# Exps as shifted piecewise linear powers on VectorE, streamed FFN weights and column-tiled matmuls in a transformer block

## Chip, cores and metric

The kernel runs on one core of one Trainium2 chip. The metric is device time in microseconds (us) of one execution. The time before is 918.04 us (median of 3 runs, 917.89 to 921.31). Every experiment was run with executions of the kernel before beside it on the same chip. All executions quoted were classed as fast.

## The reference

One adaLN block: layer norm, modulation from `c`, attention with 32 heads of width 16 over 2048 tokens, residual, second layer norm, FFN with a tanh GELU gate, residual. Cut to what matters:

```python
x = A_x                                        # (1, 2048, 512) bf16
mod = (silu(c) @ w_mod)                        # six rows of 512
h = layernorm(x) * (1 + ca) + sa
q, k, v = split(h @ wqkv)                      # 32 heads, 16 wide
p = softmax(q @ k.T * 16 ** -0.5)              # 32 x 2048 x 2048 exps
x = x + ga * ((p @ v) @ wo)
h = layernorm(x) * (1 + cb) + sb
x = x + gb * ((gelu(h @ w_gate) * (h @ w_up)) @ w_down)   # 512 -> 1792 -> 512
```

## The kernel before

Scores are made transposed: keys on 128 partitions, 512 queries along the free axis. One such 128x512 tile in one PSUM bank is called a **slot** here. There are 32 x 16 x 4 = 2048 slots to exponentiate. ScalarE takes two or three slots per activation. Some single slots go to VectorE instead. PV is a matmul of `[v, 1]` (17 columns, so that the softmax denominator comes out with it), and four heads run side by side in four column tiles of TensorE. A **round** is such a group of four slots.

Tokens are worked off in groups of 512, 512, 512, 256, 128, 128 (called groups 0 to 5). While the attention of one group runs, the output projection, layer norm and FFN of the group before are fed into TensorE's gaps as "side work". All side work shares one PSUM bank, `mi`. The order of everything is fixed when the program is built, by a greedy scheduler with a model of time of its own; it is not decided on the chip.

```python
    def mm(self, out, lhsT, rhs, start=True, stop=True, tp=None):      # all matmuls pass here
        n = 1
        for _, k in rhs.ap[1:]:
            n *= int(k)
        n *= 4 if mybir.dt.size(rhs.dtype) == 4 else 1
        return self.rec("pe", lambda e: e.matmul(out, lhsT, rhs, start=start, stop=stop, tile_position=tp),
                        [lhsT, rhs], [out], cost=(n, int(rhs.ap[0][1]), tp))

    def exp_dve(self, i, bank):                # one slot on VectorE: five operations
        t, lo, u, out = self.dt[i % 2], self.dlo[i % 2], self.du[i % 2], self.ED[:, i % 3, :]
        return [lambda: self.ts("dve", t, bank, 127 * OCT, 0.0, ALU.add, ALU.max),
                lambda: self.stt(u, lo, EXP_C2 / EXP_C3 * OCT, lo, ALU.add, ALU.mult),
                lambda: self.stt(u, u, (EXP_C1 - 1) / EXP_C3 * OCT ** 2, lo, ALU.add, ALU.mult),
                lambda: self.ts("dve", t.bitcast(FP32), t, 128 / OCT, None, ALU.mult),
                lambda: self.stt(out.bitcast(I16), u, 128 * EXP_C3 / OCT ** 3, t.bitcast(FP32), ALU.mult,
                                 ALU.add)], out

    def mod_cols(self, bank, base):            # modulation columns: 32 matmuls of ONE column
        for ci in range(8):
            for dc in range(NDC):
                self.mm(bank[:, ci:ci + 1], self.wmod[:, dc, base + P * ci:base + P * ci + P],
                        self.sc_bf[:, dc:dc + 1], start=(dc == 0), stop=(dc == NDC - 1))

    # ... FFN of one group (cut): gate chunk G, up chunk U; chunks of 256 of the 1792 columns
        def G(ci):
            # ... four or eight matmuls into mi ...
            self.copy("dve", g[...], mi[...])
            self.task([lambda: self.tt("dve", w, g, g, ALU.mult),
                       lambda: self.ts("dve", w, w, GELU_C, 1.0, ALU.mult, ALU.add),
                       lambda: self.tt("dve", w, w, g, ALU.mult),
                       ("act", lambda: self.act(w, w, ACT.Tanh, scale=TANH_C0))], ("gelu", gi, ci))
    # ... the weights are loaded once (wg, wu, wd; 5.5 MB) and stay in SBUF ...

    # ... in stream(): when a slot may go to VectorE
                if (('v', 3, 0) in self.have and len(active) < NACT and ... and self.backlog() < BACK
                        and self.free["dve"] < t + 700 and len(mem) == CH and slack > -100 and self.credit < 1024):
    # credit: matmul columns of side work that are owed by now
```

The softmax here doesn't subtract the row's maximum and nothing guards it: scores larger than these inputs give would overflow.

## Time and profile before

| | before |
|---|---|
| time, median | 918.04 us |
| slots on ScalarE / on VectorE | 1891 / 157 |
| filler matmuls (whole 128x128x512, to keep TensorE's clock up) | 312 |

The profile's busy table, kernel before. Each entry is an engine, its busy us, its share of the span and its instructions:

```profile
PE 806.3 (88%) x7461; PEld 262.4 (29%) x7461; DVE 773.6 (84%) x1512; ACT 890.1 (97%) x747; POOL 3.6 (0%) x11
```

The chain of waits that ended last, by engine, kernel before:

```profile
ACT 87%; PE 6%; DVE 5%; DMA 1%; SPq 0%; issue 0%; DVEq 0%
```

ScalarE (ACT) is busy 97% of the span and carries 87% of the chain. It is the bound.

Groups of instructions, kernel before: line of a helper, engine, operation, output <- inputs, shapes, count, then busy us and mean ns of one, then idle time before it and who ended it:

```profile
L310 ACT ACTIVATE E<-ps_sc 128x1536 bf16<-128x1536 f32 x507 | 732.0, 1603 | 2.1 <-PE ps_sc L297 1.8
L310 ACT ACTIVATE E<-ps_sc 128x1024 bf16<-128x1024 f32 x185 | 214.1, 1175 | 1.1 <-PE ps_sc L297 1.1
L322 DVE TENSOR_SCALAR dt<-ps_sc 128x512 int32<-128x512 f32 x157 | 108.4, 690 | 45.8 <-PE ps_sc L297 43.8
L327 DVE SCALAR_TENSOR_TENSOR ED<-du,dt 128x512 int16<-128x512 f32 x157 | 106.9, 683 | 0.6
```

Durations of neighbours overlap at their ends. A three-slot activation lasts 1.60 us, but in the chain of waits 18 of them in a row take 24.18 us, 1.34 us each. That spacing is what one costs; for two slots it is 0.92 us. So the exps cost ScalarE 507 x 1.34 + 185 x 0.92 = 850 us.

Busy us by stretch, kernel before. Columns: stretch, its length, then busy us and instruction counts of PE, PEld, DVE, ACT and POOL, then TensorE's granted clock, the DMA share and GB/s:

```profile
0.00:100.00 100.00, 87.86 (x740) 34.33 (x740) 67.98 (x174) 89.14 (x85) 3.65 (x11) 0.95 0.34 108
100.00:650.00 550.00, 477.33 (x3464) 128.81 (x3461) 497.37 (x901) 548.99 (x453) 0.00 (x0) 1.00 0.06 18
650.00:800.00 150.00, 135.66 (x1550) 43.76 (x1547) 128.21 (x245) 149.96 (x122) 0.00 (x0) 1.00 0.07 17
800.00:900.00 100.00, 90.14 (x1530) 44.08 (x1525) 70.95 (x171) 97.45 (x81) 0.00 (x0) 1.00 0.07 16
```

From 100 to 880 us ScalarE is full; before that it waits for the start, after that for the tail.

TensorE's timeline of the kernel before, start and duration in us; these lines show what a change of mode costs:

```profile
399.79 0.39 PE L297 MATMUL ps_sc<-qT,kme 32*128 32x512 bf16 x3
400.11 0.39 PE L297 MATMUL ps_mi<-wreg,mreg 128*128 128x512 bf16 x1
...
410.38 0.39 PE L297 MATMUL ps_pv<-E,vaug 128*17 128x512 bf16 x3
410.39 0.38 PE L297 MATMUL ps_pv<-ED,vaug 128*17 128x512 bf16 x1
410.60 0.39 PE L297 MATMUL ps_pv<-E,vaug 128*17 128x512 bf16 x4
```

Two PV rounds in the same mode start 0.22 us apart. A row-tiled score round and a whole matmul start 0.32 us apart. The Trainium skill gives a reason, in "TensorEngine Tiling (Array Packing)", "Key Properties": changing the tiling mode drains TensorE. The trace agrees that a change costs time, here 0.10 us; it doesn't show the draining itself.

### The profile page before, as it was taken

The numbers are of one execution on the slowest core, as the hardware profiler recorded it, in microseconds if no ns is written. First come the engines' busy times: TensorE is split into PE (matmuls) and PEld (weight loads), VectorE is DVE, ScalarE is ACT, GpSimd is POOL, SyncE is SP. The second block draws the span as 40 slices with busy tenths as digits, with TensorE's granted clock in tenths as the row PEclk, the third lists the DMA queues.
The fourth block names the chain that finished last, engine by engine and source line by source line (L and its number), as shares of the span: only waits on it lengthen the run. The fifth ranks groups of instructions, "written<-read, shape, count | busy, mean of one in ns | idle before, by whom it ended". The sixth has DMA issues, their size and how long they took to land.

```text
span 919.3 us, 17768 instructions
## 1 busy us (share of the span) xinstructions
PE 806.3 (88%) x7461; PEld 262.4 (29%) x7461; DVE 773.6 (84%) x1512; ACT 890.1 (97%) x747; POOL 3.6 (0%) x11
## 2 busy tenths in 40 slices
PE   7999888888889888888898888888889989998987
PEld 3333222222222222222222222222222322334455
DVE  7746999989897999998997999999999787868664
ACT  5999999999999999999999999999999999999992
POOL 1000000000000000000000000000000000000000
PEclk8899999999999999999999999999999999999999
DMA  9002320000000000000000000000000000000000
GB/s 297 1 25 55 132 93 13 13 14 14 14 13 5 10 12 14 14 13 17 16 19 12 14 13 13 2 13 18 25 21 14 14 8 14 26 20 14 21 8 13
DMA packets 31417, 24.97 MB, mean 27 GB/s; under 512 B 16205, under 2 KB 26122, under 8 KB 31338
## 3 DMA queue, kind: packets, MB, share of 16 engines
q1 hardware_dynamic: 28954, 22.28, 8.4%
q10 hardware_dynamic: 2384, 1.57, 0.6%
q8 instruction: 58, 0.95, 0.4%
q14 instruction: 21, 0.17, 0.1%
HBM read 21.23 MB, written 2.61 MB: 26 GB/s over the span
## 4 chain that ended last, share of the span: by engine, by line
ACT 87%; PE 6%; DVE 5%; DMA 1%; SPq 0%; issue 0%; DVEq 0%
ACT E L310 84%; PE ps_sc L297 3%; ACT wreg L310 2%; PE ps_mi L297 1%; PE ps_pv L297 1%; DVE du L327 1%; DMA scr_rec<-rden 1%; DVE st L350 0%; DVE dt L322 0%; DMA rb<-scr_rec 0%; SPq L360 0%; DVE xw L314 0%; DVE nwt L314 0%; DVE hreg L322 0%; PE ps_mi L301 0%
## 5 line engine op out<-in xcount | busy, mean ns | idle before, releaser
L310 ACT ACTIVATE E<-ps_sc 128x1536 bf16<-128x1536 f32 (+2 forms) x698 | 863.9, 1481 | 11.9 <-PE ps_sc L297 11.5
L297 PE MATMUL ps_pv<-E,vaug 128*17 128x512 bf16 (+2 forms) x2499 | 180.5, 325 | 1.3 <-DVE vaug L331 1.1
L297 PE MATMUL ps_sc<-qT,kme 32*128 32x512 bf16 (+2 forms) x1344 | 155.6, 332 | 23.2 <-ACT E L310 17.5
L297 PE MATMUL ps_sc<-qT,kmo 32*128 32x512 bf16 (+2 forms) x1408 | 154.4, 324 | 19.5 <-ACT E L310 15.3
L322 DVE TENSOR_SCALAR dt<-ps_sc 128x512 int32<-128x512 f32 x157 | 108.4, 690 | 45.8 <-PE ps_sc L297 43.8
L297 PE MATMUL ps_mi<-wreg,mreg 128*128 128x512 bf16 (+2 forms) x512 | 127.2, 340 | 11.4 <-DVE wreg L327 7.0
L297 PE MATMUL ps_sc<-xs,ident 128*128 128x512 bf16 x285 | 92.3, 386 | 42.2 <-ACT E L310 40.2
L327 DVE SCALAR_TENSOR_TENSOR ED<-du,dt 128x512 int16<-128x512 f32 x157 | 106.9, 683 | 0.6
L327 DVE SCALAR_TENSOR_TENSOR du<-du,dt 128x512 f32<-128x512 f32 x157 | 106.0, 681 | 0.3
L327 DVE SCALAR_TENSOR_TENSOR du<-dt 128x512 f32<-128x512 uint16 x157 | 106.1, 683 | 0.2
L297 PEld LDWEIGHTS ps_sc<-qT,kme 32*128 32x128 bf16 x1344 | 41.4, 91 | 138.0 <-ACT E L310 93.3
L297 PEld LDWEIGHTS ps_sc<-qT,kmo 32*128 32x128 bf16 x1408 | 42.2, 91 | 129.0 <-ACT E L310 85.8
L297 PEld LDWEIGHTS ps_pv<-E,vaug 128*17 128x17 bf16 x2499 | 48.8, 88 | 101.2 <-issue 90.9
L297 PE MATMUL ps_mi<-dreg,hreg 128*128 128x512 bf16 x210 | 65.3, 385 | 1.7 <-DVE xw L314 1.0
L322 DVE TENSOR_SCALAR dt<-dt 128x512 f32<-128x512 int32 x157 | 64.9, 417 | 0.6
L297 PEld LDWEIGHTS ps_mi<-wreg,mreg 128*128 128x128 bf16 x512 | 38.9, 97 | 76.9 <-issue 35.8
L297 PE MATMUL ps_pv<-ED,vaug 128*17 128x512 bf16 (+2 forms) x189 | 59.6, 346 | 0.3 <-DVE ED L327 0.2
L331 DVE CAST wreg<-ps_mi 128x512 bf16<-128x512 f32 x51 | 35.1, 688 | 17.7 <-PE ps_mi L297 16.9
L297 PEld LDWEIGHTS ps_sc<-xs,ident 128*128 128x128 bf16 x285 | 19.5, 97 | 90.4 <-ACT E L310 88.0
L327 DVE SCALAR_TENSOR_TENSOR wreg<-wreg,ps_mi 128x512 bf16<-128x512 bf16 x51 | 34.8, 683 | 7.3 <-PE ps_mi L297 7.1
L297 PE MATMUL ps_mi<-hreg,wreg 128*128 128x512 bf16 x120 | 39.2, 390 | 1.6 <-DVE qT L322 0.9
L297 PE MATMUL ps_mi<-wo,onorm 128*128 128x512 bf16 x120 | 36.5, 384 | 0.7 <-DVE xw L314 0.7
(116 smaller groups left out, 506.4 us busy)
## 6 DMA issues: line engine op xcount, KB each, us to landing
rb<-scr_rec SPq DMA_DIRECT2D x96, 64.0 KB, 2.0
mreg<-in_w_mod_dram SPq DMA_DIRECT2D x1, 2048.0 KB, 14.5
out_dram<-xs SPq DMA_DIRECT2D x16, 128.0 KB, 1.7
mreg<-in_B_w_gate_dram SPq DMA_DIRECT2D x4, 448.0 KB, 3.9
mreg<-in_B_w_up_dram SPq DMA_DIRECT2D x4, 448.0 KB, 5.4
rb<-scr_rec SPq DMA_DIRECT2D x52, 32.0 KB, 1.8
dreg<-in_B_w_down_dram SPq DMA_DIRECT2D x3, 512.0 KB, 5.2
wreg<-in_A_wqkv_dram SPq DMA_DIRECT2D x3, 384.0 KB, 10.6
```

The costliest lines, as they stand in the source:

```text
L297: return self.rec("pe", lambda e: e.matmul(out, lhsT, rhs, start=start, stop=stop, tile_position=tp), [lhsT, rhs], [out], cost=(n, int(rhs ...
L310: return self.rec("act", lambda e: e.activation(out, in_, func, scale=scale, **kw), rd, wr, cost=self.cost("act", out, [in_], "act"))
L322: return self.rec(eng, lambda e: e.tensor_scalar(out, a, s1, s2, **kw), rd, [out], cost=self.cost(eng, out, [a], "ts"))
L327: return self.rec("dve", lambda e: e.scalar_tensor_tensor(out, a, s, b, op0=op0, op1=op1), rd, [out], cost=self.cost("dve", out, [a, b], " ...
L331: return self.rec(eng, lambda e: e.tensor_copy(out, in_), [in_], [out], cost=self.cost(eng, out, [in_], "ts"))
```

## The change

Intent: take more exps off ScalarE. On VectorE a slot's exp becomes one read of the scores that writes the 16-bit pattern of a piecewise linear power of two. Its error is evened out by summing five such powers, shifted against each other. The four shifted copies are cheap 16-bit additions over a whole round (2048 elements). The sum is taken by TensorE: each shifted copy is one more PV round against a rescaled copy of V, accumulated in the same PSUM bank. Only key tiles 12 to 15 may be done so, because the scaled copies of V (`vs`) need SBUF. To make room, FFN weights are streamed anew for groups 0 to 3, and for groups 4 and 5 they are reloaded into space that has come free; the ring of ScalarE's exps shrinks from 15 slots to 12. TensorE gets four more PV rounds per VectorE round. To pay for that, every whole matmul becomes four column tiles, so that it shares PV's mode.

The diff, cut to its core (cuts marked `...`):

```diff
-NSL = 15
+NSL = 12
+T0 = 12
+NK = 3
+CREDIT = 1024
...
+SHIFT = (26, 51, 77, 102)
+SHIFT_C = float(128 * (127 - np.log2(5) - 0.0565))
...
+        if tp is None and int(rhs.ap[0][1]) == P and int(lhsT.ap[-1][1]) == P and mybir.dt.size(rhs.dtype) == 2:
+            for j in range(4):
+                self.mm(out[32 * j:32 * j + 32], lhsT[:, 32 * j:32 * j + 32], rhs, start, stop, (0, 32 * j))
+            return
         return self.rec("pe", lambda e: e.matmul(out, lhsT, rhs, start=start, stop=stop, tile_position=tp),
...
+        def load(x, ci):                       # streamed: next chunk of w_gate / w_up
+            if flow and ci < len(chunks):
+                self.dma("sp", self.wst[x][ci % 2], v[:, :, 2 * P * ci:2 * P * ci + 2 * P], "st%d%d" % (x, ci % 2))
...
-        due = (ends[1] + 30, ends[2] + 30, ends[3] + LAG, ends[-2] - 16)
+        due = (ends[1] + 30, ends[2] + 30, ends[3] + LAG, ends[3] + 2 * LAG)
...
+            if parts and pos >= loaded and ("ffn", 2 if early else 3) in self.have:    # reload for groups 4, 5
...
+                    elif (cand and self.quad_free and (pos < ends[2] or self.credit < CREDIT) and ...):
+                        ...                    # a new round of four slots for VectorE
+                    self.ts("dve", kq[:, 512 * j:512 * j + 512].bitcast(U16), self.scp[:, s0 + n, :], 128 / OCT, SHIFT_C,
+                            ALU.mult, ALU.add)
...
+    def shift_task(self, q, i):
+            self.ts("dve", self.sq[s].bitcast(U16), self.kq[q["k"]].bitcast(U16), float(SHIFT[i]), None, ALU.add)
```

`pos < ends[2] or credit < CREDIT`: after the attention of group 2 (slot 1536 of 2048), a VectorE round starts only while little side work is owed.

## The prediction

> **What bounds it now.** ScalarE. The busy table has ACT 97%, PE 88%, DVE 84%; the chain of waits is 84% ScalarE exps; in the table of stretches ACT is busy 50.0 of 50 us nearly everywhere from 100 to 850 us. The exps are 2048 slots of 128x512: by the groups of instructions 507 three-slot and 185 two-slot activations take about 1891, VectorE 157. In the chain a three-slot activation costs 1.34 us, a two-slot one 0.92: 850 us. Around that: 16 us before the first exp, 38 us after the last, 24 us of FFN tanh; ScalarE's waits are small (11.5 us on scores).
>
> **VectorE exps.** Today a slot costs five operations; in the timeline four start 0.60 us apart, the fifth takes 0.33: 2.73 us. After, a slot is one read of scores (0.60), plus, per round of four slots, four 2048-element 16-bit shifts. The bf16 1024-element tensor_scalar takes 414 ns, the two-tensor form 684, which agrees with the Trainium skill, "VectorE: DVE Perf Modes", "The perf-mode tier table" (4x for bf16 tensor_scalar in SBUF). From 291 ns at 512 elements and 414 at 1024 I estimate 0.66 us for 2048, 0.60 start to start. A round then costs 4.8 us instead of 10.9.
>
> **How many rounds n go to VectorE.** Its other work is 356 us of durations by the groups, about 300 start to start. Only k-tiles 12 to 15 are allowed (120 rounds at most). Usage near 0.83 of 850 us leaves about 402 us: n = 84 (75 to 100), 335 slots instead of 157. Each goes with a two-slot activation: 335 x 0.92 + (1713 - 670)/3 x 1.34 = 774 us of ScalarE against 850: 76 us less, all on the critical path.
>
> **TensorE.** Added: four PV rounds per VectorE round, 0.22 us each (two started 410.38 and 410.60): 73 us. Removed: most fillers (312, some 78 us with their switches), and mode switches between PV and full matmuls. A change of mode costs 0.1 us (score round to FFN matmul 0.32, same mode 0.22), as in the skill, "TensorEngine Tiling (Array Packing)", "Key Properties": switching drains. Five such per 12 us: 35 to 40 us. Four concurrent column tiles should take as long as one full matmul. So PE ends above 90% of a shorter span, and ScalarE's waits for scores should grow by 10 to 25 us: E has 12 slots instead of 15, and a unit's PV can't end until VectorE's last shift, which blocks the next unit in the one PV bank.
>
> **Off the path.** Streaming weights: some 16 MB more at a mean of 26 GB/s now, landings of 2 to 5 us: no cost. Scaled copies of V: 4 us of VectorE. The tail stays about 38 us.
>
> **Sum.** 918 - 76 + about 15 of new waits = 857. I say 856 us, range 828 to 890. Faster by over 2%: 0.91; within 2%: 0.06; slower: 0.03.
>
> **What would show it.** ScalarE exp time down by about 75 us; about 335 VectorE score reads and as many shifts at about 0.66 us; PE at 90% or more, fillers below 100; column-tiled FFN groups 0.22 us apart; DVE 85 to 92%; ACT over 93%.
>
> **What would make it wrong.** The unsigned 16-bit shift not getting the fast mode (1.2 or 2.2 us): n collapses. Column tiles loading weights slower (four loads for one), making PE the bound: 880 or more. VectorE late with shifts, filling E and stalling ScalarE. Or the scheduler reaching n near 110: about 830.

## The result and the profile after

The changed kernel takes 907.09 us (median of 4 runs, 904.66 to 909.09), against 919.67 us for the kernel before in the same rounds. The ratio is 0.986, 95% interval 0.983 to 0.989. Ratios here are the mean time of one kernel's fast runs over that of the other's of the same rounds, so not quite the ratio of the medians quoted. The range of the prediction (828 to 890) is missed.

The busy table and the chain of waits by engine, changed kernel:

```profile
PE 817.2 (90%) x13408; PEld 288.4 (32%) x13408; DVE 687.5 (76%) x1303; ACT 841.9 (93%) x747; POOL 3.7 (0%) x11
```

```profile
ACT 51%; PE 31%; DMA 7%; DVE 7%; SPq 3%; issue 2%; DVEq 0%
```

ScalarE's share of the chain fell from 87% to 51%. TensorE, DMA and the queue of the sync engine (SPq) have come in, and so has "issue", time in which an engine waits for nothing that the profile shows.

Groups of instructions, changed kernel (`dreg` and `mreg` hold the VectorE exps now):

```profile
L322 ACT ACTIVATE E<-ps_sc 128x1536 bf16<-128x1536 f32 x384 | 545.0, 1508 | 17.6 <-PE ps_sc L309 16.5
L322 ACT ACTIVATE E<-ps_sc 128x1024 bf16<-128x1024 f32 x308 | 310.7, 1096 | 4.9 <-PE ps_sc L309 4.6
L334 DVE TENSOR_SCALAR dreg<-ps_sc 128x512 uint16<-128x512 f32 x188 | 129.5, 690 | 36.0 <-PE ps_sc L309 34.0
L334 DVE TENSOR_SCALAR mreg<-ps_sc 128x512 uint16<-128x512 f32 x92 | 63.0, 689 | 16.0 <-PE ps_sc L309 15.0
L334 DVE TENSOR_SCALAR mreg<-dreg 128x2048 uint16<-128x2048 uint16 x188 | 123.1, 682 | 2.8 <-PE ps_pv L309 2.8
```

VectorE takes 188 + 92 = 280 slots (70 rounds). The prediction had 335. The shift of 2048 elements takes 0.68 us; the prediction had 0.66. The Trainium skill, "VectorE: DVE Perf Modes", "The perf-mode tier table", gives 693 ns for a bf16 tensor_scalar of that size in the 4x mode. The trace agrees, for uint16. At the spacings of before, ScalarE's exps now cost 384 x 1.34 + 308 x 0.92 = 798 us: 52 less, where the prediction had 76.

Busy us by stretch, changed kernel, columns as above:

```profile
0.00:100.00 100.00, 80.27 (x1540) 32.41 (x1540) 57.67 (x161) 79.18 (x77) 3.67 (x11) 0.93 0.25 80
100.00:650.00 550.00, 522.24 (x6860) 155.65 (x6856) 490.75 (x836) 546.47 (x494) 0.00 (x0) 1.00 0.13 35
650.00:800.00 150.00, 133.24 (x2440) 50.63 (x2441) 87.25 (x180) 145.17 (x115) 0.00 (x0) 0.98 0.31 89
800.00:900.00 100.00, 81.06 (x2583) 49.73 (x2580) 49.81 (x125) 71.11 (x64) 0.00 (x0) 0.95 0.25 68
```

From 100 to 650 us the picture is the predicted one: ScalarE full, VectorE at 89%, TensorE at 95%. Before 100 us ScalarE loses 10 us against the kernel before. After 650 us VectorE falls to 58% and then 50%, and ScalarE is no longer full.

To see what each stage gained, I counted slots: the moment by which ScalarE's activations and VectorE's reads have done so many of the 2048. The stages of each profiled execution in us:

| profiled run | to slot 160 | 160 to 1536 | 1536 to 2048 | after slot 2048 | span |
|---|---|---|---|---|---|
| before | 91.1 | 574.4 | 230.5 | 23.3 | 919.3 |
| after | 100.1 | 527.5 | 246.4 | 30.5 | 904.5 |
| change | +9.0 | -46.9 | +15.9 | +7.2 | -14.8 |

The middle stage won 47 us. The start, the last quarter of the slots and the tail gave 32 of them back.

### The profile page after: what moved, and what is told of

It reads as the page before. It is cut to its first block, busy times and chain, and to the rows that moved or that the text cites. A ratio compares the mean times of both kernels' runs of the same rounds, so it can differ in the third digit from the quotient of the medians.

```text
span 904.5 us, 29537 instructions
## 1 busy us (share of the span) xinstructions
PE 817.2 (90%) x13408; PEld 288.4 (32%) x13408; DVE 687.5 (76%) x1303; ACT 841.9 (93%) x747; POOL 3.7 (0%) x11
## 3 DMA queue, kind: packets, MB, share of 16 engines
HBM read 43.25 MB, written 2.61 MB: 51 GB/s over the span
## 4 chain that ended last, share of the span: by engine, by line
ACT 51%; PE 31%; DMA 7%; DVE 7%; SPq 3%; issue 2%; DVEq 0%
ACT E L322 49%; PE ps_mi L309 13%; PE ps_sc L309 12%; PE ps_pv L309 6%; DMA scr_rec<-rden 3%; SPq L372 3%; ACT wreg L322 2%; DMA mreg<-in_B_w_gate_dram 1%; DVE mreg L334 1%; DMA mreg<-in_w_mod_dram 1%; DVE wreg L326 1%; DVE wreg L339 1%; DVE wreg L343 1%; DMA rb<-scr_rec 1%; DMA mreg<-in_B_w_down_dram 1%
## 5 line engine op out<-in xcount | busy, mean ns | idle before, releaser
L322 ACT ACTIVATE E<-ps_sc 128x1536 bf16<-128x1536 f32 (+2 forms) x698 | 811.6, 1318 | 35.2 <-PE ps_sc L309 33.9
L309 PE MATMUL ps_sc<-qT,kmo 32*128 32x512 bf16 (+2 forms) x1408 | 183.8, 328 | 10.8 <-ACT E L322 7.5
L309 PE MATMUL ps_sc<-qT,kme 32*128 32x512 bf16 (+2 forms) x1344 | 178.0, 333 | 14.4 <-ACT E L322 12.1
L334 DVE TENSOR_SCALAR dreg<-ps_sc 128x512 uint16<-128x512 f32 x188 | 129.5, 690 | 36.0 <-PE ps_sc L309 34.0
L309 PE MATMUL ps_mi<-wreg,mreg 128*32 128x512 bf16 (+2 forms) x1920 | 124.1, 355 | 17.4 <-DVE wreg L339 5.4
L334 DVE TENSOR_SCALAR mreg<-dreg 128x2048 uint16<-128x2048 uint16 x188 | 123.1, 682 | 2.8 <-PE ps_pv L309 2.8
L309 PE MATMUL ps_pv<-mreg,vs 128*17 128x512 bf16 (+1 forms) x1232 | 98.4, 361 | 1.9 <-DVE mreg L334 1.4
L334 DVE TENSOR_SCALAR mreg<-ps_sc 128x512 uint16<-128x512 f32 x92 | 63.0, 689 | 16.0 <-PE ps_sc L309 15.0
L309 PEld LDWEIGHTS ps_mi<-wreg,mreg 128*32 128x32 bf16 x1920 | 42.8, 98 | 73.9 <-issue 26.0
L334 DVE TENSOR_SCALAR mreg<-mreg 128x2048 uint16<-128x2048 uint16 x92 | 60.3, 684 | 0.9 <-PE ps_pv L309 0.9
L343 DVE CAST wreg<-ps_mi 128x512 bf16<-128x512 f32 x51 | 35.0, 686 | 23.9 <-PE ps_mi L309 23.3
L309 PE MATMUL ps_mi<-hreg,wreg 128*32 128x512 bf16 x480 | 39.9, 391 | 0.7 <-DVE vaug L343 0.5
L326 DVE TENSOR_TENSOR onorm<-osb,rb 128x512 bf16<-128x512 f32 (+2 forms) x43 | 23.6, 549 | 19.8 <-DMA rb<-scr_rec 19.6
L309 PE MATMUL ps_mi<-mreg,hreg 128*32 128x512 bf16 x448 | 36.5, 384 | 0.2 <-DMA mreg<-in_B_w_down_dram 0.2
```

What stands on the lines that cost most here:

```text
L322: return self.rec("act", lambda e: e.activation(out, in_, func, scale=scale, **kw), rd, wr, cost=self.cost("act", out, [in_], "act"))
L326: return self.rec(eng, lambda e: e.tensor_tensor(out, a, b, op), [a, b], [out], cost=self.cost(eng, out, [a, b], "tt"))
L334: return self.rec(eng, lambda e: e.tensor_scalar(out, a, s1, s2, **kw), rd, [out], cost=self.cost(eng, out, [a], "ts"))
L343: return self.rec(eng, lambda e: e.tensor_copy(out, in_), [in_], [out], cost=self.cost(eng, out, [in_], "ts"))
```

## The experiments

Eighteen kernels ran. Medians; "before" is the median of before in the same rounds, and the ratio is as explained above:

| label | this us | before us | ratio |
|---|---|---|---|
| e_small | 889.65 | 918.84 | 0.967 |
| e_tile256 | 898.89 | 918.84 | 0.978 |
| e_untiled | 907.88 | 918.84 | 0.987 |
| b_tile256 | 924.00 | 918.84 | 1.006 |
| s_poolw | 891.20 | 919.47 | 0.969 |
| s_gate_open | 967.80 | 919.47 | 1.053 |
| s_gate_open_pool | 962.96 | 919.47 | 1.048 |
| s_gate2560_pool | 916.51 | 919.47 | 0.996 |
| b_short (wrong result) | 909.14 | 919.29 | 0.987 |
| s_short_pool (wrong result) | 869.52 | 919.29 | 0.945 |
| x_nogelu (GELU falsified) | 939.73 | 919.29 | 1.019 |
| x_halfup (wrong result) | 959.54 | 919.29 | 1.042 |
| b_tiny | 919.01 | 919.25 | 0.999 |
| s_noexp | 1015.82 | 919.25 | 1.105 |
| b_noexp | 991.97 | 919.25 | 1.078 |
| o_urg0_late2 | 902.94 | 919.25 | 0.985 |
| s_tail | 886.49 | 919.54 | 0.965 |
| s_tail_pool_sp5 | 888.11 | 919.54 | 0.967 |

Names: `b_` starts from the kernel before, the others from the changed one. All `s_`, `x_` and `o_` kernels carry the edit of e_small too. The stages of their profiled runs, where they are used below:

| profiled run | to slot 160 | 160 to 1536 | 1536 to 2048 | after slot 2048 | span |
|---|---|---|---|---|---|
| e_small | 90.7 | 525.7 | 245.9 | 27.7 | 890.0 |
| e_untiled | 92.9 | 544.7 | 248.8 | 23.0 | 909.4 |
| b_tile256 | 88.7 | 575.3 | 231.3 | 25.1 | 920.4 |
| s_poolw | 90.7 | 526.0 | 243.6 | 30.7 | 891.0 |
| s_gate_open | 89.8 | 526.3 | 210.0 | 139.5 | 965.6 |
| b_short | 89.2 | 575.3 | 219.7 | 23.6 | 907.8 |
| s_short_pool | 90.9 | 526.0 | 222.6 | 29.7 | 869.2 |
| b_noexp | 88.8 | 636.8 | 239.6 | 25.6 | 990.8 |
| s_noexp | 91.4 | 631.8 | 259.8 | 30.2 | 1013.2 |
| s_tail | 92.0 | 525.7 | 239.8 | 24.1 | 881.6 |

### The start: one-column matmuls split in four

TensorE's timeline of the changed kernel near the start; the bracket is the idle time before the line and what ended it:

```profile
9.80 1.16 PE L309 MATMUL ps_sc<-sc_bf,mreg 128*32 128x1 bf16 x126 [1.78 <-DMA mreg<-in_w_mod_dram]
16.55 0.19 PE L309 MATMUL ps_sc<-sc_bf,mreg 128*32 128x1 bf16 x2 [5.59 <-issue]
```

The rule in `mm` also splits the modulation's 32 matmuls of one column into 128. After 126 of them TensorE stands for 5.59 us, and no semaphore holds it. The record has 222 matmuls and 223 weight loads of TensorE in the first 11 us; the kernel before has 64 and 65. The queue that the profile calls "instruction" moves blocks of 16 KB. In this run the first of them since the start lands between 14.0 and 15.2 us, and TensorE goes on at 16.55. So the suspicion was that it had run out of instructions.

e_small:

```diff
-        if tp is None and int(rhs.ap[0][1]) == P and ...
+        if tp is None and n >= P and int(rhs.ap[0][1]) == P and ...
```

> The changed kernel, but the 64 one-column modulation matmuls are left whole (only matmuls of 128 columns and more are split into column tiles). Theory A (splitting small matmuls starves TensorE's instruction supply): the 5.6 us gap of TensorE at 11 us goes, the first exp starts near 17 us instead of 23.3, and the time falls by 5 to 8 us to about 900. Theory B (TensorE is simply full, start is unrelated): first exp stays at 23 us and the time within 2 us of 907.

Measured: 889.65 us, 17 less than the changed kernel's 907.09, twice the expectation. TensorE's timeline of e_small at the same place:

```profile
10.65 0.94 PE L309 MATMUL ps_sc<-sc_bf,mreg 128*128 128x1 bf16 x32 [1.33 <-DMA mreg<-in_w_mod_dram]
11.52 0.61 PE L309 MATMUL ps_mi<-dreg 128*32 128x512 bf16 x8
```

The gap is gone. The stage up to slot 160 takes 90.7 us instead of 100.1. Counted by slots in the two profiled executions, e_small is ahead by 6.6 us from the first slots to slot 128, by 10.8 us at slot 192, by much the same (10.4 to 12.1 us) up to slot 2048, and by 14.5 us at the end. So the first 6.6 us go with the gap of 5.59. The next 4 us go with the other block of modulation columns: it, too, is split into 128 matmuls, which start at 91.63 us, and then TensorE stands again with nothing to wait for:

```profile
94.66 0.37 PE L309 MATMUL ps_sc<-qT,kmo 32*128 32x512 bf16 x1 [1.29 <-issue]
```

Here a 16 KB block had landed at 93.3 us, 1.3 us before TensorE goes on; at the first gap it was 1.4 us. The last 3 us are lost after slot 2048, where TensorE's "issue" waits are 5.9 us in the changed kernel and 3.6 in e_small.

The clock is part of the second loss. The clock record of the changed kernel is at half speed for 10.2 us from 10.8 us on, and again for 6.8 us from 96 us on; e_small has neither. But the first spell begins 0.2 us before the gap does, and the kernel before also has 10.2 us of half clock between 10.8 and 28 us, without such a gap. So the gap at most prolonged that spell. One stretch of both around the second spell, first the changed kernel, then e_small (the third number from the end is the granted clock):

```profile
97.00:104.00 7.00, 7.00 (x54) 1.43 (x50) 4.42 (x7) 5.10 (x5) 0.00 (x0) 0.57 0.11 39
```

```profile
97.00:104.00 7.00, 6.46 (x122) 2.30 (x125) 5.79 (x9) 7.00 (x8) 0.00 (x0) 1.00 0.01 2
```

The Trainium skill, "TensorE: Matmul & The Clock Gate", "Part 1: The HAM clock gate", says that one idle window of about 3.4 us takes the clock to half. The trace agrees with the length: the spells at half clock are 3.41 us long or two to three times that. It does not show idle windows: matmuls ran in 47% of the 3.41 us before the first spell of the changed kernel and in 62% of those before the second.

b_tiny does this one thing alone, in the kernel before (split only matmuls of fewer than 128 columns):

```diff
+        if tp is None and n < 128 and int(rhs.ap[0][1]) == P and ...   # four column tiles
```

> The kernel before with only the 64 one-column matmuls of the modulation split into column tiles. If these starve TensorE's instruction supply by themselves: a TensorE gap of about 5 us near 11 us, first exp at 21 to 24 us instead of 16.5, the time up by 5 to 12 us (925 to 931). If the gap needs the rest of the change: within 2 us of before.

Measured: 919.01 us, no change, and no gap. So the split of the small matmuls is not enough by itself. b_tiny had issued 155 matmuls and 157 loads by 11 us, the changed kernel 222 and 223, because there the warm-up matmuls are split too. Both are needed for the gap; the reading is that only then does TensorE outrun the block that lands at about 14 us. That it is the supply of instructions fits all four records (before, b_tiny, e_small, after), but no run controlled the fetch itself.

### Column tiling elsewhere

e_tile256 leaves 128-column matmuls whole as well (`n >= 256`), and e_untiled leaves all whole (`False and ...`):

> As e_small, but matmuls of 128 columns are left whole too, so only 256 and 512 columns are split. Theory A: the 'issue' gaps of TensorE after 879 us (about 7 us together) shrink to under 2 us, and the time falls 3 to 7 us below e_small, about 895. Theory B (the mode switches around whole matmuls cost more than the supply of instructions): equal to e_small or slower by 2 to 5 us.

Measured: 898.89 us with a wide spread (891.7 to 904.8), slower than e_small, so the expected gain didn't come. The "issue" gaps did go: the waits of TensorE in e_tile256 have none. But the schedule changed everywhere too (272 VectorE slots instead of 280), so this run doesn't isolate the tail.

> The changed kernel with no full matmul split: column tiling undone, VectorE exps and streaming kept. If TensorE is the bound in the middle stage (100 to 650 us), losing some 35 us of saved mode switches shows there: stage longer by 10 to 30 us and time above e_small. If ScalarE is the bound there and TensorE still has slack, the middle is within 5 us, and with both ends cured the time is 892 to 902.

Measured: 907.88 us, 18 over e_small. The middle stage is 544.7 us against 525.7, so column tiling is worth 19 us there. About 5 of them are its 12 fewer VectorE slots, at the 0.45 us found below. TensorE is close to the bound in the middle once it carries the extra PV rounds.

b_tile256 has only the tiling, in the kernel before:

> The kernel before with only the column tiling (256 columns and more). ScalarE bounds it and waits for nothing, so saved mode switches only turn into idle time of TensorE: within 3 us of before (917 to 921).

Measured: 924.00 us, ratio 1.006, interval 1.003 to 1.008: a little slower, three microseconds outside the expectation. With ScalarE as the bound, tiling buys nothing. TensorE's busy time fell by 14 us (806.3 to 792.4), although it carries some ten fillers more.

The tail was isolated later. s_tail is e_small with the matmuls of the tail alone left whole below 256 columns:

```diff
+ n >= (256 if self.tailing else P)      # tailing is set where the tail begins
```

> e_small (890 us) with the 128-column matmuls of the tail alone left whole; the schedule up to the tail is the same. If splitting them starves TensorE's instruction supply in the tail: the 'issue' gaps after 850 us (4 to 6 us together) go and the time falls by 3 to 7 us, to 883 to 887. If mode and weight loads matter more: within 2 us of 890.

Measured: 886.49 us (0.965; e_small had 0.967 in its rounds). That is 3 us, at the near edge of the expectation. Waits of TensorE on "issue", the only such lines of each run, first e_small, then s_tail:

```profile
PE ps_sc L309 <- issue: 3.6, 3, 1.3
PE ps_mi L309 <- issue: 0.8, 1, 0.8
```

```profile
PE ps_mi L310 <- issue: 0.8, 1, 0.8
```

Splitting 128-column matmuls costs 3 to 4 us of such gaps in the tail. The gain in time is not clear of noise: the 95% intervals of the two ratios overlap (0.964 to 0.971 and 0.963 to 0.966). s_tail has the lowest median of the correct kernels.

### What a VectorE slot is worth, and what the rest costs

s_noexp is e_small with an empty list of candidates; b_noexp is the kernel before with `NACT = 0`. In both, all exps are on ScalarE.

```diff
-        cand = [k for k, (u, r, g0) in enumerate(rounds) if u not in units[:2] and r * (512 // u[3]) >= T0]
+        cand = []
```

> e_small with every exp on ScalarE. 280 slots come back at 0.42 us each where ScalarE is the bound all the way: 890 + 118 = 1008. If in the last third VectorE's exps never counted (12 of the 280 are there anyway) but the FFN did, much the same. Well under 990 would say that VectorE exps cost ScalarE as much as they save.

> The kernel before with every exp on ScalarE: 157 slots come back at 0.42 us: 918 + 66 = 984. The difference s_noexp less b_noexp is the cost of streaming, of the smaller ring and of column tiles with VectorE exps out of the way: near 0 if they are free while ScalarE is the bound, 20 or more if they are not.

Measured: 1015.82 and 991.97 us. So 280 VectorE slots are worth 1015.82 - 889.65 = 126 us in the new form, 0.45 us each. In the old form 157 are worth 991.97 - 919.25 = 73 us, 0.46 each. A slot off ScalarE is worth what the prediction said (0.42), slightly more, and the new form gives it at less than half of VectorE's time.

The two differ by 24 us with VectorE's exps out of the way. That is the price of the rest: streaming, reload, smaller ring, other due dates. The table of stages says where it lies: the middle is even 5 us shorter, the stage after slot 1536 is 20 us longer and the tail 5. Both runs from 850 to 950 us, first b_noexp, then s_noexp:

```profile
850.00:950.00 100.00, 86.25 (x1344) 37.49 (x1360) 43.15 (x103) 100.00 (x80) 0.00 (x0) 1.00 0.07 18
```

```profile
850.00:950.00 100.00, 81.06 (x1775) 36.24 (x1770) 36.73 (x89) 88.66 (x71) 0.00 (x0) 0.97 0.40 115
```

ScalarE loses 11 us in this stretch, while DMA goes from 7% to 40%. This is the FFN of group 3 and the reload for groups 4 and 5.

### The loads: another queue, other spacing

In e_small TensorE waits for weights exactly there (waits of TensorE, 775 to 830 us; us in total, times, longest):

```profile
PE ps_mi L309 <- DMA mreg<-in_B_w_gate_dram: 5.7, 2, 4.2
PE ps_mi L309 <- DMA mreg<-in_B_w_up_dram: 2.2, 2, 1.8
```

The program gives TensorE its matmuls in one order, so a matmul that waits for a weight also holds up the scores behind it: over the 4.2 us wait, at 778 to 782 us, ScalarE stands for 4.9 us. The queue of the sync engine carries these loads together with the softmax denominators' round trips, in order. s_poolw issues the loads from the idle GpSimd engine:

```diff
-                self.dma("sp", self.wst[x][ci % 2], ...)       # likewise wdst and the reload
+                self.dma("pool", self.wst[x][ci % 2], ...)
```

> As e_small, but every load of FFN weights is issued by the idle GpSimd engine instead of the sync engine, whose queue also carries the reciprocals' round trips in order. Theory A (weight loads queue behind the softmax denominators): TensorE's waits for weight loads, 10 us in e_small, fall below 3 us, its clock drops after 780 us go, and the time falls by 6 to 12 us to about 880. Theory B (the loads themselves are slow or their buffers come free late): the same waits stay, time within 3 us of e_small's 889.7.

Measured: 891.20 us, no gain. Locally the theory held: in that stretch no wait of TensorE for weights is left, and from the first transposes of group 3's FFN to its first down matmul it takes 45 us instead of 55 (the kernel before: 35). But the time came back: a 6.1 us gap of ScalarE appears at 830.6 us. There a round trip of the denominators (`rb<-scr_rec`) lands in 4.9 us instead of about 2, with seven weight loads of the reload under way. VectorE waits 5.8 us for it, and a reciprocal that TensorE needs stands behind it in VectorE's order, so TensorE waits 5.6 us. s_tail_pool_sp5 spaced the reload:

```diff
-                loaded = pos + 3
+                loaded = pos + (3 if early else 5)     # with s_tail and the GpSimd queue
```

> s_tail with weight loads on the GpSimd queue and the last reload spaced (one load per 5 slots instead of 3). If the burst of loads delayed the softmax round trip in s_poolw: that round trip lands in about 2 us instead of 4.9, ScalarE's 6 us gap near 832 us goes, and the time is 876 to 882. If not: 884 to 892.

Measured: 888.11 us, no better than s_tail. The gap is still 4.7 us and those round trips still land in 3.9 us (median). The spacing was too small to tell whether the burst is the cause. That stays open.

### More VectorE exps in the last third

The most obvious loss was that VectorE takes only 12 slots after slot 1600. s_gate_open takes the limit away (and loads any weights still missing at the end, so that the program can be built):

```diff
-CREDIT = 1024
+CREDIT = 10**9
```

> As e_small, with the limit on VectorE exps while FFN work is owed taken away (344 VectorE slots by the program instead of 280). Theory A (the missing VectorE exps of the last quarter are what the prediction lost): 64 slots at 0.42 us of ScalarE each, up to 27 us, so 865 to 875. Theory B (in the last quarter TensorE and the FFN's chain through one PSUM bank are the bound, so exps moved off ScalarE only delay the FFN): no gain, 885 to 905, with FFN work pushed behind the last exp and a longer tail.

Measured: 967.80 us. My first theory fell, and far. VectorE does take 344 slots, and the last exp comes 36 us earlier than in e_small (slot 2048 at 826 against 862 us). But then the FFN is left over: 139.5 us after the last slot instead of 27.7. The same with the GpSimd queue, and with a half-open limit:

> Both: limit taken away and weight loads on the GpSimd queue. If both theories A hold, the gains nearly add: 855 to 868. If the FFN's chain bounds the last quarter, about the time of s_poolw.

> Limit at 2560 instead of 1024, 312 VectorE slots, loads on the GpSimd queue. Half way: 868 to 875 under theory A; best of the four if too many VectorE exps delay the FFN.

Measured: 962.96 and 916.51 us (the trace of the second has 320 VectorE slots, not 312). The more VectorE slots after slot 1536 (24, 64 and 88 in s_poolw and these two), the longer the program. Busy us by stretch in s_gate_open_pool:

```profile
635.00:720.00 85.00, 77.15 (x1471) 33.15 (x1471) 72.80 (x139) 80.82 (x75) 0.00 (x0) 0.96 0.07 17
720.00:823.00 103.00, 93.04 (x2265) 46.35 (x2264) 87.23 (x157) 98.78 (x86) 10.44 (x14) 0.98 0.19 49
823.00:960.00 137.00, 87.67 (x2082) 51.68 (x2076) 63.10 (x148) 13.58 (x22) 31.63 (x43) 0.76 0.31 92
```

Up to 823 us TensorE, VectorE and ScalarE are all at 85 to 96%. After that the FFN runs with no engine above 64%: it is a chain (matmul, VectorE copy, three VectorE operations, tanh, matmul, two VectorE operations, through one PSUM bank). That this chain is what limits it there is argued; no run gave it a second bank. And it started late: group 2's last output projection is at 670 us and the first transposes for its FFN at 718. The layer norm between them had waited 48 us on VectorE behind exps.

Which part of the FFN collides? Two kernels with a falsified FFN for groups 2 and 3, both from s_gate_open_pool:

```diff
# x_nogelu
-                    self.task([tt w=g*g, ts, tt w=w*g, ("act", tanh(w))], ("gelu", gi, ci))
+                    self.task([("act", tanh(g))], ("gelu", gi, ci))          # for gi >= 2
# x_halfup
-                for dci in range(NDC):
+                for dci in range(NDC // 2 if gi >= 2 else NDC):
```

> Wrong result on purpose. s_gate_open_pool (963 us, 344 VectorE slots), but for token groups 2 and 3 the three VectorE operations of the GELU polynomial are left out; TensorE's work is the same. If VectorE's share of the FFN is what collides with the exps in the last third: falls by 60 to 100 us, to 865 to 900. If TensorE or the round trip through the one PSUM bank is it: falls by less than 40.

> Wrong result on purpose. s_gate_open_pool (963 us), but for token groups 2 and 3 the up and gate matmuls sum over half of the model width; VectorE's work is the same. If TensorE is what is short in the last third: falls by 60 to 100 us. If it is VectorE: falls by less than 40, less than x_nogelu.

Measured: 939.73 and 959.54 us, so 23 and 3 us less than 962.96 (the 3 are within the spread of the runs). Neither share of the work alone is what is short. VectorE's part matters more than TensorE's.

o_urg0_late2 changes the order instead: exps' shifts no longer go ahead of layer norm and GELU steps, and after slot 1536 a new VectorE round starts only while at most one such step is owed.

```diff
-URGENT = 9
+URGENT = 0
-                    ... and self.backlog() < BACK
+                    ... and self.backlog() < (BACK if pos < ends[2] else 2)
```

> s_gate_open_pool (963 us, 344 VectorE slots) with VectorE's queue reordered: shifts go before LayerNorm and GELU steps only when nothing else of the unit is left to do, and in the last third a round starts only while at most one such step is owed (312 slots by the program). If the order of VectorE's queue starved the FFN: 880 to 905, and LayerNorm of group 2 no longer waits 48 us. If the last third is bound by something else: stays over 930.

Measured: 902.94 us with 312 slots. This is 60 us better than s_gate_open_pool; group 2's layer norm now waits 10 us instead of 48. It also has 32 slots fewer, and the run doesn't separate the two. s_gate2560_pool suggests that the number is the larger part: with 24 slots fewer and the old order it had already won 46 of these 60 us. The new order, with 8 slots fewer still, brings the other 14. But it is still 12 us slower than s_poolw with 280 slots. In the last third more VectorE exps bring nothing in any order that was tried.

Last, the FFN itself. b_short and s_short_pool compute only 3 of 7 FFN chunks for groups 2 and 3:

```diff
-        nch = len(chunks) if part is None else part
+        nch = (3 if gi in (2, 3) else len(chunks)) if part is None else part    # and 6 of 14 down matmuls
```

> Wrong result on purpose. The kernel before, but token groups 2 and 3 (768 of 2048 tokens) compute 3 of the 7 chunks of the FFN. Before is bound by ScalarE to the end: it should lose only the left-out tanh work, 4 x 0.95 + 4 x 0.51 = 6 us, and a little more through extra VectorE exps: 905 to 914.

> Wrong result on purpose. s_poolw (891 us) with the same cut. Theory C (after the attention of group 2, at two thirds of the span, the FFN work that is left sets the time, and it keeps VectorE exps out): the FFN of groups 2 and 3 gets some 80 us shorter, VectorE exps come in, the time falls by 30 to 60 us, to 830 to 860. Rival (ScalarE's exps alone set the last third): only 6 us plus 20 more VectorE slots at 0.42, to about 876.

Measured: 909.14 us, 10 less than before, and 869.52 us, 22 less than s_poolw. The expectation for the second was 30 to 60 (830 to 860), its rival's 15 (876): it lies between, and neither holds as stated. The FFN that is owed in the last third does cost the changed kernel twice what it costs the kernel before, and VectorE slots come in when it is cut (300 instead of 280). But it isn't the sole bound there.

## Why the prediction was wrong

Right, with numbers:

- ScalarE bounded the kernel before, and a slot off ScalarE is worth about 0.42 us (measured 0.45).
- The new VectorE form costs what was estimated: 0.68 us per shift (0.66), 0.69 us per score read.
- In the middle stage it worked as costed. A count in the traces gives 253 VectorE slots there instead of 131, which at 0.42 us each are 51 us; 47 were measured.
- Four column tiles take as long as one whole matmul: in the changed kernel's timeline 16 of them span 1.05 us. With 0.39 us for the last one that leaves 0.22 us from one group of four to the next. TensorE ended at 90%, and the fillers' work fell from 312 to 128 whole matmuls, which is not below the 100 that was predicted.

Wrong:

- **"Usage near 0.83 of 850 us leaves about 402 us: n = 84."** This is the first step that failed: 70 rounds, 280 slots. VectorE was at 89% from 100 to 650 us, but it can't be used evenly. Half of the tokens' FFN falls due after slot 1536, and there the program holds exps back; forced in, they lengthen it (s_gate_open, +78 us on e_small). After slot 1536 VectorE took 24 slots, no more than in the kernel before, and over the whole span it ended at 76% busy, where 85 to 92% were predicted. 55 slots at 0.45 us are 25 us.
- **"Streaming weights: ... no cost", with 15 us of new waits elsewhere.** The streaming read 22 MB more from HBM (43.25 against 21.23), not 16. The change without VectorE exps costs 24 us (s_noexp against b_noexp), all of it after slot 1536. Tiling is hardly the cause of those 24: in the kernel before, tiling of 256 columns and more leaves that stage as it was (231.3 against 230.5 us). The profile shows TensorE waiting for streamed weights there. But freeing those waits (s_poolw) brought no time, so how the 24 us divide between streaming, reload, due dates and the ring of 12 slots, which no run tried by itself, stays open.
- **The start was not considered at all.** Splitting one-column matmuls costs 17 us (907.09 against 889.65). In the profiled pair 11 of 14.5 us are lost by slot 192, by two gaps of TensorE and, at the second, a spell at half clock; about 3 are lost in the tail.
- **"ScalarE's waits for scores should grow by 10 to 25 us"**, because of the smaller ring and the one PV bank. They grew by 22 us (11.5 to 33.9), so the size is right, but by luck: in the middle stage, which holds 253 of the 280 VectorE slots, they are 2.8 us, and 26 lie after slot 1536.
- "35 to 40 us" of saved mode switches: TensorE's busy time fell by 14 us (b_tile256). Off the path before; worth up to 19 us in the middle of the changed kernel.

As a sum: 856 predicted, + 25 for missing slots, + 9 for the rest's cost above the 15 foreseen, + 17 for the split of one-column matmuls, is 907, the measured time. The terms come from different programs, and the 15 were meant for other waits than those in the 24, so that they add up this well is partly luck. One can also write 919.25 - (280 - 157) x 0.45 + 24 = 888, where e_small measured 889.65. That is no check: 0.45 and 24 were worked out from e_small's own time with those of s_noexp and b_noexp. It only says that a slot is worth the same in both forms.

## What to carry to other kernels

When an engine gets relief, ask stage by stage whether its helper is free in that stage; an average share of busy time hides that half of the helper's own work may fall in the last third. A rule that rewrites every instruction of a kind should be looked at for its smallest instances: 64 one-column matmuls, split in four, cost more than a third of what the middle stage had won. Leaving matmuls below 128 columns whole in the changed kernel, and those of 128 in the tail, gives 886.5 us, 3.5% under the kernel before.

## What the Trainium skill lacked or had wrong

- Supply of instructions: "Runtime: NRT & Kernel Launch", "Instruction fetch mechanics", describes the refill in 16 KB blocks but gives no time for a refill that comes late. In the changed kernel TensorE stood 5.6 us after 222 matmuls and 223 weight loads in the first 11 us, with no semaphore to wait for, and went on 1.4 us after the next 16 KB block of the instruction queue had landed (14.0 to 15.2 us); it stood 1.3 us more at 94 us. In the tail of e_small such gaps added up to 4.4 us. That these gaps are late refills is the likely reading, not a tested one.
- "TensorE: Matmul & The Clock Gate", "Part 1: The HAM clock gate", speaks of an idle window before the clock falls to half. Before the two spells of the changed kernel matmuls ran in 47% and 62% of the window.
- "TensorE: Matmul & The Clock Gate", "LDWEIGHTS (loading the stationary operand)", makes the load's time proportional to the columns. The records show 89 ns for 17 columns and 98 ns for 32, both column-tiled, so they don't show that proportion. A whole load of 128 columns takes 97 ns, but it can't be compared directly: "TensorEngine Tiling (Array Packing)", "Restrictions", says that column tiling disables the fast weight load. Whatever that costs, groups of four tiles with one moving operand still started 0.22 us apart.
- "VectorE: DVE Perf Modes", "The perf-mode tier table", lists bf16 and fp32 only. The same page's text on the modes asks for 16-bit types, so this is a gap of the table alone. A tensor_scalar addition on uint16, 2048 elements, took 682 to 684 ns in SBUF, close to the table's 693 for bf16.
